# Six slot plans of a fused RWKV-6 and GELU-MLP kernel, each put in a new order

## The chip, the cores and the metric

The kernel runs on one core of a Trainium2 chip. Its time is the device time of one execution in microseconds (us), and the figure for a kernel is the median of several runs. A profile is a separate execution, recorded by the hardware. The engines are PE (TensorE, the matrix engine; PEld is its weight load), DVE (VectorE), ACT (ScalarE), POOL (GpSimd) and SP (SyncE, which here issues nearly all DMAs). Every engine works through its own queue of instructions in the order in which the program recorded them, and waits at an instruction until what it needs is there.

## The reference

First comes a linear-attention recurrence over 768 time steps for 4 batches and 8 heads of 48 channels, in float32:

```python
for t in range(S):
    cur = einsum('bhd,bhe->bhde', u * k[t], v[t])
    y[t] = einsum('bhd,bhde->bhe', r[t], state + cur)
    state = w[t][..., None] * state + einsum('bhd,bhe->bhde', k[t], v[t])
```

The heads are then laid side by side to a matrix `x` of 3072 rows and 384 columns, and an MLP follows with the exact GELU: `gelu(x @ w_in) @ w_out`, 384 to 2048 to 384.

## The kernel before, in words

The 3072 rows are cut into eight blocks of 384 (T), two for each batch; block `x` is half `x % 2` of its batch. Attention of a block works on chunks of 64 steps (C). Its output `xT` is the input of the MLP of the same block. The two are pipelined: in stage `x` (L1390 to L1416) the MLP of block `x - 1` is recorded together with the attention of block `x`, and the last MLP stands alone behind the stages.

**Slots and plans.** `attention(x, unit)` (L366 ff) and `mlp(x)` (L982 ff) are Python generators. Each `yield` ends a slot, which is a handful of instructions. `PLAN[x]` is a string that stands in the source; each letter takes the next slot from one stream and so records its instructions next on their engines:

```python
streams = {".": mlp(x - 1), "s": slots, "f": following, "l": load(x + 1, nc.sync), ...}
for c in PLAN[x]:
    next(streams[c], None)
for c in ".slxw" if x == 0 else ".slxwc":
    while next(streams[c], streams) is not streams:
        pass
slots = following
```

`.` is the MLP, `s` the rest of this block's attention, `f` the start of the next block's attention, `l` the loads of the next block, `x` five or ten sums of `xT` that the next MLP needs, `w` sums of weights (stages 2 and 7 only). A letter whose stream is at its end does nothing. Slots of one stream keep their order, so a plan only decides how the streams are interleaved, and with that the order in every engine's queue. "Stage 2" to "stage 7" below go by the key of the plan; they are the third to eighth stage.

**The attention slots of blocks 2 to 7**, with the names used in this document:

| name | work | lines |
|---|---|---|
| A0 | four products r*u*k on DVE; needs the loads of r and k | L404 |
| A1 to A11 | products and sums on DVE over r, k and the decays w | L391, L398, L424, L432 |
| Q0 | ACT copies r (plain), DVE scales it into `kx` (lay out) | L573, L578, L579 |
| Q1, Q2, Q4 | three bursts of 64x64 matmuls into pairs of PSUM banks (`d`); Q4 also has small ones | L604, L595 |
| Q3, Q9, Q10 | DVE copies the three bursts under masks into `a_sb` | L637 |
| Q5, Q6, Q7 | DVE updates r and k; Q6 has the ACT copies for Q8 | L658, L665, L669, L573 |
| Q8 | lay out again, for the second round | L578, L579 |
| Q11, Q12 | two masked DVE copies of the small matmuls | L687 |
| R1, R2, R4 | the bursts of the second round; in even blocks R1 holds all three | L604 |
| R3, R10, R11 | ACT copies their rows, six or twelve copies each | L620 |
| R5 to R7 | DVE updates r and k | L658, L665, L669 |
| R8, R9 | four DVE transposes of k and then twelve small DMAs, the moves, on SP (eight and four) | L552, L547 |
| K1 | four ACT copies of k's diagonal blocks | L733 |
| KV | 64x64 matmuls of k and v, into both pairs of banks | L749 |
| S1 to S3 | 20 DVE steps that chain the states out of these banks | L764 |
| I | matmuls into `y_ps` (both pairs again), and a fence: a tiny DVE copy | L790, L802 |
| Y | more matmuls into `y_ps`, held behind the fence; six ACT copies and six DMAs to `xT` | L832, L855, L862 |

There are two pairs of banks, used in turn. So a burst waits until the copies of the burst before the last are done, I waits for the end of S3, and R4 waits for R3.

**The MLP slots.** `h_halves` (L1011 to L1083) computes the hidden layer with seven products for each of four groups of blocks; its slots are called first, third, seventh, second, fifth, sixth and fourth, and run for q = 0 to 3. Each has four or eight 192-column matmul records, an ACT copy or GELU, and in third and seventh a DVE addition (L1065, L1083). Then come the output products (L1237), two slots of eight records each, in this order: 00, 11, 01, s2, s1, s3, s2w. After them an odd block has five more products (E11, Es2, Es1, Es3, Es2w; L1342 to L1360) and an even one two (al0, al1; L1331, L1334). `of_g` (L1003 to L1007) makes sums of GELUs on DVE. The hidden slots and the products share two PSUM banks, so the first slots of a stage wait until the last products of the stage before have been added or copied (L1360, L1334).

Q0 to Q12 of a stage are among its `s`; A0 to A9 may come as `f` of the stage before. Loads have ten slots: three for r, three for w, three for k and one for v, 256 KB each but the last.

Of the kernel before, what the change touches and what calls it, by code (L numbers as in the profile page):

```python
# [41 lines left out]
        ".cswc.ccc.cccss.lc.ccscs..cc.cs.cclwcsc.ccssc.c.cccsccc..ssccc.c.lcls.cc.ccsc.w.clwscclccc"  # L42
        ".c.swcw.ss.ccs.lcsc..cwcccslccslff..w..fw.wfs..f..flffffffww"
    ),
    2: "...l...s..ws.swssswssss.sslsw...ssss.sssws.ll..ws.w..lw.sw.wl.sls.sls..lf.s....sf..f.f.xx.fxl.x.x",
    3: "l..sss..s.s..s.s....s...s.ssllss.sss.s.s.ss.l..lsss..sssss.sls.s..s......s..ls.llssf.sf.sflf.f.x.x..xxfffxf",
    4: "...s...lsl......s.s....sss..ssss..s..ss..s..s...llssslss....s.slss...s...sll.sl.s.sfs..fsf.ff..xl.x.xfffxffx",
    5: ".l..........ls.ss...s.sslls.ssss..ss.sls...sss..sssssl.ss.s..s.......s.lssll.sfsf.f.s.ff.x..x.xxxl",
    6: "sss.sls.....s......ls.s....s.sssssss..s.....s.ss....s.s.ssss.s.l.ss.l.ls.l...s.l.lslssf..s.ffs..lff.xx..xffxffx",
    7: "......s.s....s.s...s.ssssss...sss.ss...sss..ssss.s...ss.ww.ww.wwsw.ww.ww.ws.s.ss.s.ww.swww.swwwwwwww.wwww.www.xxxx.xxxxxx",  # L50
}


# [1423 lines left out]
```

## Time and profile before

| what | us |
|---|---|
| median of 3 runs (588.08 to 589.55) | 589.5 |
| the profiled execution | 592.28 |
| its span, first to last instruction | 590.5 |
| PE busy | 571.7 (97%) |
| DVE busy | 462.9 (78%) |
| ACT busy | 275.9 (47%) |
| mean granted TensorE clock | 1.000 |

The span is the time from the first to the last instruction on the core; the execution takes 1.8 us more. A matmul in float32 is recorded as two matmuls, and their recorded ends overlap, so the distance from one start to the next says more than the duration: 192 columns follow each other every 0.163 us. Some records are missing.

### The profile page before, as it was taken

How to read it: one execution, taken by the hardware profiler on the slowest of the kernel's cores; microseconds unless marked ns; L12 is line 12 of the kernel's file. 1: busy time of each engine (PE TensorE's matmuls, PEld its weight loads, DVE VectorE, ACT ScalarE, POOL GpSimd, SP SyncE). 2: the span in 40 equal slices, each digit the busy share in tenths (PEclk: the TensorE clock that was granted, in tenths of full speed). 3: DMA queues.
4: the chain of work that ended last, by engine and by line, in shares of the span. 5: the costliest groups of instructions: out<-in, count | busy, mean ns of one | idle time of the engine just before them, and what ended most of it. 6: DMA issues, size and time to landing. Idle time of an engine off the chain costs nothing. (4 is left out here: it accounts for less than half of the span.)

```text
span 590.5 us, 17425 instructions
## 1 busy us (share of the span) xinstructions
PE 571.7 (97%) x7505; PEld 508.1 (86%) x7517; DVE 462.9 (78%) x907; ACT 275.9 (47%) x640; POOL 8.0 (1%) x21
## 2 busy tenths in 40 slices
PE   7769999999999999999999999999999999999998
PEld 3566666766799999999999999999998999999997
DVE  7879767988968986787859987688758998975532
ACT  2458889323612558046461468145560465523400
POOL 3100000000000000000000000000000000000000
PEclk9999999999999999999999999999999999999999
DMA  7649661120142301341023311330015200210000
GB/s 245 206 138 354 211 232 56 34 88 2 29 139 78 109 3 31 98 125 38 1 42 104 122 38 21 93 115 7 3 31 163 73 2 2 41 39 8 1 14 33
DMA packets 51004, 46.80 MB, mean 79 GB/s; under 512 B 31728, under 2 KB 36080, under 8 KB 50928
## 3 DMA queue, kind: packets, MB, share of 16 engines
q1 hardware_dynamic: 50832, 45.62, 25.4%
q8 instruction: 59, 0.97, 0.7%
q14 instruction: 17, 0.14, 0.1%
q10 hardware_dynamic: 96, 0.07, 0.1%
HBM read 36.24 MB, written 4.72 MB: 69 GB/s over the span
## 5 line engine op out<-in xcount | busy, mean ns | idle before, releaser
L1011 PE MATMUL h_ps<-xT,w_in_sb 128*128 128x192 f32 x408 | 81.2, 330 | 0.7 <-DVE o_sb L1360 0.6
L1011 PEld LDWEIGHTS h_ps<-xT,w_in_sb 128*128 128x128 f32 x408 | 67.8, 190 | 3.7 <-ACT g L1043 1.2
L1223 PE MATMUL h_ps<-xT,w_in_sb 128*128 128x384 f32 x192 | 64.1, 490 | 0.1
L1223 PEld LDWEIGHTS h_ps<-xT,w_in_sb 128*128 128x128 f32 x192 | 35.9, 190 | 23.9
L1237 PE MATMUL o_ps<-w_out_sb,g 128*128 128x192 f32 x224 | 39.5, 326 | 0.0
L1237 PEld LDWEIGHTS o_ps<-w_out_sb,g 128*128 128x128 f32 x224 | 36.9, 190 | 0.3
L620 ACT COPY a_sb<-d 32x256 f32<-32x256 f32 (+8 forms) x90 | 32.6, 362 | 4.6 <-PE d L604 3.1
L1237 PE MATMUL o_ps<-w_out_sb,f 128*128 128x192 f32 x176 | 31.7, 330 | 0.0
L1237 PE MATMUL o_ps<-t,g 128*128 128x192 f32 x176 | 31.4, 329 | 0.0
L1237 PE MATMUL o_ps<-w_out_sb,e 128*128 128x192 f32 x176 | 31.3, 328 | 0.0
L1237 PE MATMUL o_ps<-t,s 128*128 128x192 f32 x176 | 30.9, 327 | 0.0
L1237 PE MATMUL o_ps<-t,e 128*128 128x192 f32 x176 | 30.9, 327 | 0.0
L637 DVE COPY_PREDICATED a_sb<-quarter,d 128x480 f32<-128x480 uint8 (+5 forms) x54 | 23.1, 437 | 8.6 <-PE d L604 7.3
L465 PEld LDWEIGHTS d<-rkw 64*64 64x64 f32 x1152 | 19.1, 134 | 12.2 <-issue 8.5
L764 DVE SCALAR_TENSOR_TENSOR st<-st,tot_sb,kv_ps 128x48 f32<-128x48 f32 x160 | 28.9, 257 | 0.9 <-PE kv_ps L749 0.8
L1011 PE MATMUL u_ps<-s,w_in_sb 128*128 128x192 f32 x160 | 29.5, 327 | 0.0
L1237 PEld LDWEIGHTS o_ps<-t,g 128*128 128x128 f32 x176 | 28.7, 190 | 0.4
L1237 PEld LDWEIGHTS o_ps<-w_out_sb,e 128*128 128x128 f32 x176 | 28.8, 190 | 0.3
L1237 PEld LDWEIGHTS o_ps<-w_out_sb,f 128*128 128x128 f32 x176 | 28.7, 190 | 0.4
L1237 PEld LDWEIGHTS o_ps<-t,s 128*128 128x128 f32 x176 | 28.8, 190 | 0.1
L1237 PEld LDWEIGHTS o_ps<-t,e 128*128 128x128 f32 x176 | 28.8, 190 | 0.1
L604 PE MATMUL d<-kx,rkw 64*64 64x96 f32 x1056 | 28.2, 248 | 0.0
(236 smaller groups left out, 1163.6 us busy)
## 6 DMA issues: line engine op xcount, KB each, us to landing
rkw<-in_rkw_dram SPq DMA_DIRECT2D x54, 256.0 KB, 4.0
raw<-in_w_out_dram SPq DMA_DIRECT2D x8, 768.0 KB, 5.2
v_in<-in_v_dram SPq DMA_DIRECT2D x8, 584.0 KB, 4.1
raw<-in_w_in_dram SPq DMA_DIRECT2D x5, 768.0 KB, 8.8
out_dram<-o_sb SPq DMA_DIRECT2D x20, 192.0 KB, 2.2
rkw<-kx SPq DMA_DIRECT2D x72, 48.0 KB, 2.0
rkw<-in_rkw_dram SPq DMA_DIRECT2D x6, 384.0 KB, 5.7
raw<-in_w_in_dram SPq DMA_DIRECT2D x9, 256.0 KB, 3.3
```

What stands on the lines that cost most here:

```text
L465: nc.tensor.matmul(d[half[p], g, n * width:(n + 1) * width], lhsT=kc[half[g], b, i, p], rhs=right(half[g], b, i, p), start=True, stop=True)
L604: nc.tensor.matmul(o[half[p], i * 3 * C // 2:(i + 1) * 3 * C // 2], lhsT=kc[half[g], n // NI, n % NI, p], rhs=rx[half[g], 2 * n + p], star ...
L620: nc.scalar.copy(out=at[z, g, first:behind, (a + 1) * h:], in_=d[z, :, :, to] if g == slice(None) else d[z, :, to])
L637: nc.vector.copy_predicated(out=an[:, :, :, :, (a + 1) * h:], mask=mask.to_broadcast(data.shape), data=data)
L764: nc.vector.scalar_tensor_tensor(out=stq[:, q, c], in0=stq[:, q, c - 1] if c else b4[:, q, NC - 1], scalar=totq[:, q, c:c + 1], in1=kvs[q ...
L1011: nc.tensor.matmul(o, lhsT=lhsT, rhs=rhs, start=start, stop=True, skip_group_check=True)
L1223: nc.tensor.matmul(h_ps, lhsT=w_in_sb[:, f // FI, j, f % FI * 128:(f % FI + 1) * 128], rhs=xT[:, j, :], start=(j == 0), stop=(j == NJ - 1))
L1237: nc.tensor.matmul(o, lhsT=lhs(j), rhs=rhs(j), start=start and j == 0, stop=(j == HF - 1), skip_group_check=True)
```

## The change

Six strings of `PLAN` are replaced. Every stream still gives the same slots in the same order, and the letters `f` are as many in each plan as before (5, 9, 10, 5 and 9 in stages 2 to 6), so no slot changes its stage. The new strings contain a few letters (`c`, and `w` in stages 3 to 6, and some behind the end of a stream) that find an empty stream and record nothing. Two slots that the old plan of stage 2 left to the loop behind it, and one of stage 7, are now named in the plan.

```diff
-    2: "...l...s..ws.swssswssss.sslsw...ssss.sssws.ll..ws.w..lw.sw.wl.sls.sls..lf.s....sf..f.f.xx.fxl.x.x",
-    3: "l..sss..s.s..s.s....s...s.ssllss.sss.s.s.ss.l..lsss..sssss.sls.s..s......s..ls.llssf.sf.sflf.f.x.x..xxfffxf",
-    4: "...s...lsl......s.s....sss..ssss..s..ss..s..s...llssslss....s.slss...s...sll.sl.s.sfs..fsf.ff..xl.x.xfffxffx",
-    5: ".l..........ls.ss...s.sslls.ssss..ss.sls...sss..sssssl.ss.s..s.......s.lssll.sfsf.f.s.ff.x..x.xxxl",
-    6: "sss.sls.....s......ls.s....s.sssssss..s.....s.ss....s.s.ssss.s.l.ss.l.ls.l...s.l.lslssf..s.ffs..lff.xx..xffxffx",
-    7: "......s.s....s.s...s.ssssss...sss.ss...sss..ssss.s...ss.ww.ww.wwsw.ww.ww.ws.s.ss.s.ww.swww.swwwwwwww.wwww.www.xxxx.xxxxxx",
+    2: ".....s.ww..w.sww.wslsssssslss.l...sssssswscss...s..s..w..wwsl.ll.s.lsswls..l...ss.sff...fxfx.fxll....xxx.",
+    3: (
+        "..ssssss.....l.....llss...s.sssssss..ss..ss.l...sss.sssslss....ss......lcsssslls..s.lf.s.f"
+        "f.ff..lxx..xxffw.ffxxsl"
+    ),
+    4: (
+        "l......c......s.s..s...s...s.sss..sssslw.ssss....s.s..sll..ssss.ss.l.....sslsls..l.lsfslf."
+        "ssf...ffx..xl.xfxxffxf.f"
+    ),
+    5: "......s.....cs.s...sss.sss..s.sss.ss....sss.slssssls.s.s.....s...sllwsssl..llllfsl..fs.f....fxxf.xxsxx.l",
+    6: (
+        ".s....ss.ss.ss......s....lss.ssssss.....sllsss.......ssssssl......sss....ll.ssss..llslf.s."
+        "ff.s..ff..xx.xwfscflxxlff.x"
+    ),
+    7: (
+        ".....s...ss....s...sss.ssss.ss.sss.....lsssw..wssssssw...s..w.s...wwwscwww.sss.ws.w.swwsww"
+        ".wws.w.x.xxxxxxxxx.wwwwwwxwww.w.wwwww."
+    ),
```

## The prediction, on record before the change was run

> **What bounds the kernel now.** I read the page first, then the busy times by stage (stages 2 to 7 one below the other), then the waits of PE in that stretch, then the timeline around each wait.
>
> ```profile
> span 590.5 us, 17425 instructions
> PE 571.7 (97%) x7505; PEld 508.1 (86%) x7517; DVE 462.9 (78%) x907; ACT 275.9 (47%) x640; POOL 8.0 (1%) x21
> ```
>
> ```profile
> 120.00:192.60 72.60, 72.56 (x784) 57.79 (x785) 63.44 (x121) 24.68 (x63) 0.00 (x0) 1.00 0.23 68
> 192.60:256.90 64.30, 64.30 (x835) 61.24 (x834) 51.87 (x95) 32.35 (x84) 0.00 (x0) 1.00 0.23 60
> 256.90:329.20 72.30, 71.79 (x869) 69.19 (x868) 59.39 (x113) 33.17 (x83) 0.00 (x0) 1.00 0.22 61
> 329.20:392.80 63.60, 63.27 (x830) 60.38 (x829) 51.45 (x95) 32.32 (x84) 0.00 (x0) 1.00 0.25 68
> 392.80:465.20 72.40, 70.96 (x866) 68.42 (x865) 57.99 (x110) 33.04 (x83) 0.00 (x0) 1.00 0.23 63
> 465.20:529.90 64.70, 64.14 (x835) 61.13 (x834) 58.15 (x119) 32.42 (x84) 0.00 (x0) 1.00 0.12 32
> ```
>
> ```profile
> PE y_ps L832 <- DVE fence L802: 1.3, 1, 1.3
> PE h_ps L1011 <- DVE o_sb L1360: 0.6, 1, 0.6
> PE kv_ps L749 <- DMA rkw<-kx: 0.5, 1, 0.5
> PE y_ps L790 <- DVE st L764: 0.3, 1, 0.3
> PE h_ps L1011 <- DVE o_sb L1334: 0.2, 1, 0.2
> ```
>
> ```profile
> 42.03 0.22 DVE L800 COPY fence<-y_ps 128x1 f32<-128x1 f32 x2
> 42.30 1.38 PE L832 MATMUL y_ps<-rkw,st 64*64 64x64 f32 x39 [0.49 <-DVE fence L800]
> ...
> 219.31 2.04 PE L604 MATMUL d<-kx,rkw 64*64 64x96 f32 x80
> 220.43 2.60 ACT L620 COPY a_sb<-d 32x320 f32<-32x320 f32 x6 [0.30 <-PE d L604]
> 223.43 0.56 PE L604 MATMUL d<-kx,rkw 64*64 64x96 f32 x16
> ...
> 297.34 1.96 DVE L552 STREAM_TRANSPOSE kx<-rkw 128x384 f32<-128x384 f32 x4
> 310.52 1.74 PE L749 MATMUL kv_ps<-v_in,rkw 64*64 64x48 f32 x92 [0.51 <-DMA rkw<-kx]
> ...
> 380.30 1.63 PE L790 MATMUL y_ps<-a_sb,v_in 64*64 64x64 f32 x96 [0.33 <-DVE st L764]
> 453.93 3.01 DVE L404 SCALAR_TENSOR_TENSOR kx<-rkw,u_sb 128x384 f32<-128x384 f32 x4 [1.73 <-DMA out_dram<-o_sb]
> ```
>
> The first column pair of the stage rows is length and PE busy: over 410 us, PE is idle for 2.9 us. So the old plans already keep PE fed, and a new order can only win back the few waits listed, while each link that it tightens becomes a wait of PE. From start to start I find some 6 us in stages 2 to 7 that are not matmul pitch: Y of stage 6 1.3, KV of stage 4 0.95 and of stage 3 0.3, the starts of stages 7, 6, 4 and 3 together 1.8, I of stage 5 0.4, R2 in each odd stage 0.16, Q4 in each odd stage 0.2.
>
> **The change part by part.** Nothing is added, so only waits and mode changes count. I compared, link by link, what PE has to do between two slots with what DVE, ACT and SP need between them.
>
> *Mode changes.* Y follows I without other matmuls in stages 2 and 7; all other mergers cancel (39 runs of 64x64 matmuls become 37). Eight 192-column records between I and Y take 1.50 us instead of 1.30, and the first 64x64 load has 0.16 to 0.23 in front, so a pair costs 0.2 to 0.36: together -0.4 to -0.7, I take -0.6. [...]
>
> *I directly before Y.* The matmuls between them covered the fence. Without cover the only row is stage 0: 0.49 us of PE idle. Bounds 0.3 (the fence's 0.2 and a hand-over) and 0.7 (start to start in that row); two times 0.5, +1.0.
>
> *R4 in stages 3, 5 and 7.* R4 needs the bank of R1, which the six copies of R3 free. They start 1.12 us after R1 and last 2.60, so 3.7 us after R1. PE's cover was R1 and R2 1.8, sixth 0.65, fourth 1.3, mode change 0.2: 3.95. In stages 3 and 5 sixth now stands before R1: 3.3, late by 0.4. In stage 7 the cover stays, but Q11 and Q12 (1.92) now stand before third's addition on DVE, a GELU in second3 waits for it, and R3 behind it on ACT starts 0.9 later: late by 0.5. Bounds 0 (ACT finds slack) and 0.6; +1.3 for three. In return R2 no longer meets Q12: three times 0.16, -0.5.
>
> *I behind S.* I needs both pairs back from S3, 3.2 us after KV's end with 20 steps (stage 5: 377.10 to 380.30), 4.8 in stage 6 (447.45, S to 452.2). Stage 3 drops from 5.4 to 2.8 us of cover, +0.4. Stage 6 drops from 5.4 to 4.1, +0.7. Bounds 0 and 1.2. Stage 5 stays at its 0.4.
>
> *Stage 4.* Q1 and Q4 come 4 us later among the matmuls, R1 1.3 earlier. Q0's second half waits for ACT copies behind fourth1: Q1 late by 0.35. From Q4's end DVE then does Q6 to Q12 in 8.9 (Q8 waiting for copies behind sixth3), two additions 1.0, six sums 4.0, R5 1.35, R6 and R7 2.0, R8 1.95: 19.2. The moves take 9.3 more (twelve at 0.66, the last landing 2.0 after its issue), 28.5. PE's work from Q4 to KV is 27.2. KV so waits 1.3 in place of 0.95, and Y 0.2 behind its fence: +0.85 in all. Bounds -0.9 (DVE has slack) and +2.
>
> *Stage 5.* Between KV and A0 DVE gets L1291 (1.28). A0 ends 7.5 after KV's end, the fence at 7.7, Y is due at 7.55: +0.2. All ten loads but two now stand behind the moves on SP, so four of w and r go out just ahead of k's three. In stage 6 of before just this had k land 6.0 us after issue, against 3.3 in stage 5. I take +0.2 for it, between 0 and 1.5.
>
> *Stage 6.* R9's four moves stand behind one load only, and two loads instead of four go out before k's: A0 no longer waits 1.73, so Y's 1.3 goes. DVE is done earlier, so L1360 no longer holds stage 7: -0.7. Sum -2.0, bounds -2.1 and 0.
>
> *The rest.* KV of stage 3 lost 0.3 to moves that landed late; now K1's copies end with the last matmul before it, there and in stage 7: -0.3 and +0.1. Later loads, weight sums and A-slots I cost at nothing: the five or more matmul slots beside them cover each; without that cover a DVE slot is 0.5 to 2.4.
>
> *Sum.* -0.6 +1.0 +1.3 -0.5 +1.1 +0.85 +0.4 -2.0 -0.2 = +1.35. Two of the gains are waits after DMAs that landed 1.8 us late; such landings (306.52 to 310.38, 2.0 being usual) come in four of six stages and hit a wait twice, and can hit others: +0.65. Total +2.0. On the profiled execution (590.5 span, 592.28 in all) that is 594.3; it is 2.8 above the median, so against 589.5 I say 591.5.
>
> **The rivals.**
>
> *The ends of the stages decide: faster.* Y stands 1.3 us earlier before the stage's end in stages 3, 4 and 5, and 3.9 in stage 7, so `xT` lands and the last banks are free in time. For it: L1360 and L1334 and the late `xT` (sx0 waits 1.40 in stage 5) are what holds the starts of stages. Then all 1.8 of the starts and Y's 1.3 go, with -0.6, -0.5 and -0.95 for KV in stage 4 (-5.15), and +3.4 of R4, I and fence stays if ACT and DVE are as late as the rows say (-1.75); with two of the three R4 waits hidden +2.5 stays: -2.6, 586.9. From that point it decides. Against it: stage 5 gets A4 (2.2) between sx1 and L1334, which gives the start of stage 6 its 0.5 back.
>
> *Waits only change places: the same.* For it: every plan has the same DVE sum per stage and PE is at 99% here. Between -1.7 and +1.7; 590.
>
> *k's loads and the moves land late.* In stages 4 and 5 KV and A0 have nothing left. One late landing in each and one in stage 7 adds 1.8 each to the +1.35: 596. Against it: only two of four hit a wait before. [...]
>
> A plan that does nothing is excluded: the order of PE's and DVE's queues differs in every stage.
>
> **How the numbers follow.** My forecast, small losses between +1.8 and +4.5, has 0.40; the late landings 0.12; the same 0.28; faster 0.20. What a measurement can tell from no change is 0.3%, 1.8 us. That makes slower 0.52, same 0.28, faster 0.20. The range runs from 587.6, which cuts off about half of the faster case, to 595.0, short of the late one, and leaves out about 0.2. The slower case alone is 591.3 to 594.0.
>
> **What would show it.** R4 idle 0.3 to 0.6 before L604 in three stages; L832 idle 0.5 behind L802 in stages 2 and 7; L790 behind L764 in stages 3 and 6; KV of stage 4 behind the moves; Y of stage 6 and the start of stage 7 without a wait; PE busy time as before. It is wrong if those idle times are missing, or if a stage's start waits where I see none.

## The result and the profile after

The new order is slower. Four runs of each gave 594.39 us (592.82 to 595.21) against 589.01 (588.08 to 589.55), a ratio of 1.009 with the interval 1.0062 to 1.0118. A longer comparison, eleven runs against 34, gave 592.65 against 589.43, a ratio of 1.0052 (1.0035 to 1.0069), which is +3.1 us (2.1 to 4.1). The mean clock granted in a run does not make this difference: among its runs with 1.000 the medians are 591.89 (five) and 588.46 (eleven), among those with 0.997 they are 593.59 (six) and 589.74 (fifteen), 3.4 and 3.8 apart. The forecast was 591.5, slower by 2.0. The profiled execution of the new kernel took 593.81 us, 1.5 more than that of before.

The page's first lines, and the busy times from stage start to stage start (stages 2 to 7; a stage starts here with the first 128x192 matmul of its MLP, stage 2 with the one 128x512 matmul just before its MLP), for the new kernel; columns as in the prediction:

```profile
span 592.0 us, 17424 instructions
PE 570.4 (96%) x7505; PEld 507.5 (86%) x7517; DVE 462.6 (78%) x907; ACT 275.9 (47%) x640; POOL 8.0 (1%) x21
...
119.53:192.80 73.27, 73.05 (x787) 58.22 (x786) 62.77 (x117) 24.67 (x63) 0.00 (x0) 1.00 0.24 67
192.80:257.65 64.85, 64.06 (x834) 60.99 (x833) 52.45 (x98) 32.38 (x84) 0.00 (x0) 1.00 0.24 64
257.65:330.17 72.52, 71.34 (x867) 68.73 (x866) 58.75 (x111) 32.95 (x83) 0.00 (x0) 1.00 0.23 65
330.17:394.81 64.64, 63.77 (x833) 60.86 (x833) 51.73 (x97) 32.37 (x84) 0.00 (x0) 1.00 0.25 70
394.81:466.10 71.29, 70.92 (x866) 68.41 (x865) 58.97 (x111) 33.10 (x83) 0.00 (x0) 1.00 0.20 52
466.10:531.25 65.15, 63.83 (x834) 61.03 (x833) 57.75 (x114) 32.30 (x84) 0.00 (x0) 1.00 0.13 33
```

The busy times of all engines are those of before within 1.5 us, as they must be with the same slots; PE's idle time in the six stages went from 2.9 to 4.8 us. The waits of PE in that stretch (what waited, for whom, us in total, times, longest), and where they stand in the timeline:

```profile
PE d L616 <- ACT a_sb L632: 1.3, 3, 0.5
PE y_ps L802 <- DVE st L776: 1.0, 3, 0.4
PE y_ps L844 <- DVE fence L814: 0.9, 3, 0.6
PE kv_ps L761 <- DMA rkw<-kx: 0.6, 2, 0.4
PE y_ps L844 <- issue: 0.5, 1, 0.5
```

```profile
311.64 0.34 PE L761 MATMUL kv_ps<-v_in,rkw 64*64 64x48 f32 x9 [0.38 <-DMA rkw<-kx]
320.92 0.31 PE L844 MATMUL y_ps<-rkw,st 64*64 64x64 f32 x4 [0.56 <-DVE fence L814]
...
361.17 0.56 PE L616 MATMUL d<-kx,rkw 64*64 64x96 f32 x16 [0.39 <-ACT a_sb L632]
453.82 0.59 PE L802 MATMUL y_ps<-a_sb,v_in 64*64 64x64 f32 x25 [0.37 <-DVE st L776]
...
517.91 1.63 PE L802 MATMUL y_ps<-a_sb,v_in 64*64 64x64 f32 x96
519.72 1.02 PE L844 MATMUL y_ps<-rkw,st 64*64 64x64 f32 x48 [0.18 <-DVE fence L814]
521.19 0.93 PE L844 MATMUL y_ps<-rkw,st 64*64 64x64 f32 x48 [0.46 <-issue]
```

R4 (L616) waits for ACT's copies in stages 3, 5 and 7, I (L802) for the states (L776) in 3, 5 and 6, KV and Y in stage 4, and in stage 7 Y stops half way, 48 matmuls in, for nothing that the profile names. A line with a bracket gives idle time of PE; counted from one matmul's start to the next, less its usual pitch, the same waits are 0.1 to 0.2 longer.

### The profile page after: what moved, and what is told of

The parts are those of the page before. It is cut to its first block, busy times and chain, and to the rows that moved or that the text cites. A ratio compares the mean times of both kernels' runs of the same rounds, so it can differ in the third digit from the quotient of the medians.

```text
span 592.0 us, 17424 instructions
## 1 busy us (share of the span) xinstructions
PE 570.4 (96%) x7505; PEld 507.5 (86%) x7517; DVE 462.6 (78%) x907; ACT 275.9 (47%) x640; POOL 8.0 (1%) x21
## 4 chain that ended last, share of the span: by engine, by line
PE 58%; DVE 6%; ACT 1%; DMA 1%; issue 0%; SPq 0%; DVEq 0%
PE o_ps L1249 24%; PE h_ps L1023 15%; PE u_ps L1023 11%; PE d L616 3%; DVE st L776 2%; PE c_ps L1023 2%; PE y_ps L844 1%; ACT a_sb L632 1%; PE kv_ps L761 1%; PE y_ps L802 1%; DMA rkw<-in_rkw_dram 1%; DVE a_sb L649 1%; DVE kx L416 1%; PE d L607 0%; DMA rkw<-kx 0%
## 5 line engine op out<-in xcount | busy, mean ns | idle before, releaser
L776 DVE SCALAR_TENSOR_TENSOR st<-st,tot_sb,kv_ps 128x48 f32<-128x48 f32 x160 | 29.1, 256 | 2.3 <-PE kv_ps L761 2.2
L1238 ACT ACTIVATE g<-h_ps 128x256 f32<-128x256 f32 (+1 forms) x32 | 13.9, 433 | 31.6 <-PE h_ps L1235 31.2
L616 PE MATMUL d<-kx,rkw 64*64 64x96 f32 x1056 | 27.3, 247 | 1.3 <-ACT a_sb L632 1.3
```

The costliest lines, as they stand in the source:

```text
L616: nc.tensor.matmul(o[half[p], i * 3 * C // 2:(i + 1) * 3 * C // 2], lhsT=kc[half[g], n // NI, n % NI, p], rhs=rx[half[g], 2 * n + p], star ...
L776: nc.vector.scalar_tensor_tensor(out=stq[:, q, c], in0=stq[:, q, c - 1] if c else b4[:, q, NC - 1], scalar=totq[:, q, c:c + 1], in1=kvs[q ...
L1238: nc.scalar.activation(out=gs[group][:, f % FG, 0:t], in_=h_ps[:, 0:t], func=AF.Gelu)
```

## The experiments

**Each order once more.** The profiled execution of before was 2.8 us above its median; which of its waits does a usual execution hold? Both kernels ran again, and so did two mixtures:

```diff
-    2: ".....s.ww..w.sww.wslsssssslss.l...sssssswscss...s..s..w..wwsl.ll.s.lsswls..l...ss.sff...fxfx.fxll....xxx.",
+    2: "...l...s..ws.swssswssss.sslsw...ssss.sssws.ll..ws.w..lw.sw.wl.sls.sls..lf.s....sf..f.f.xx.fxl.x.x",
...
```

That is new357 in its first line, the new plans with 2, 4 and 6 from before; new246 has 3, 5 and 7 from before and 2, 4 and 6 new.

> The old plans unchanged, a second execution. Theory (waits of the old order come and go): the profiled execution of 592.28 held waits after late DMA landings that most executions do not hold, so this one has Y of stage 6 under 0.3 idle instead of 1.34 and the start of stage 7 under 0.4 instead of 0.72; span 586.5 to 588.5, ratio 1.000. Rival (granted clock): the waits are all there again, some 6 us in stages 2 to 7, the span is 590 to 591, and what separates the times of the two kernels is the clock granted in the timed runs (1.000 here against 0.994 for the new order).

> The new plans unchanged, a second execution. Theory: R4 waits 0.46, 0.46 and 0.62 in stages 3, 5 and 7, Y 0.5 to 0.6 behind the fence in stages 2, 5 and 7, I 0.4 behind S3 in stages 3, 5 and 6, as in the first execution, within 0.1 each, since they come from engines' fixed durations; only the two waits of KV behind the moves vary; time 594, ratio 1.009. Rival (granted clock): the same waits, but the ratio falls to about 1.003, the 1.5 us of the two first profiles, in runs where both kernels get the same clock.

> The new plans in stages 3, 5 and 7, the old ones in 2, 4 and 6. Theory: R4 waits (1.5), I behind S3 in stage 3 (0.4) and the fences of stages 5 and 7 (1.1), less R2 and the two mode changes (0.8): +2.5 over before, with those waits as long as in the new order, and stages 2, 4 and 6 as long as in the old. Rival (the stage's start decides): a stage's loss is taken over by the stage behind it, and 4 or 6 get longer by over 0.5 at their starts.

> The new plans in stages 2, 4 and 6, the old ones in 3, 5 and 7. Theory: fence of stage 2 (0.5) less two mode changes (0.3), the starts and Q1 of stage 4 (0.8), I behind S3 in stage 6 (0.4): +1.0 to +2.0 over before's typical execution, no R4 wait, R2 waits 0.16 in stages 3, 5, 7 as before. Rival (stage 6 was the loss of the old order in every execution): its 1.3 of Y and 0.7 of the start of stage 7 go, and the time is 0.5 to 1 below before.

Measured (medians; ratios to runs of before in the same comparison, with the 95% interval): before again 588.98 us (ratio 0.9984, 0.9967 to 1.0001), the new order 592.65 (1.0052, 1.0035 to 1.0069), new357 592.66 (1.0043, 1.0024 to 1.0062), new246 591.6 (1.0029, 1.0007 to 1.0050). Length of each stage in the traces, in us:

| stage | 2 | 3 | 4 | 5 | 6 | 7 | sum |
|---|---|---|---|---|---|---|---|
| before, first | 73.12 | 64.14 | 71.70 | 64.24 | 72.42 | 64.51 | 410.13 |
| before, again | 73.12 | 64.14 | 71.20 | 64.34 | 70.99 | 64.50 | 408.29 |
| new, first | 73.27 | 64.85 | 72.52 | 64.64 | 71.29 | 65.15 | 411.72 |
| new, again | 73.27 | 64.61 | 72.52 | 64.64 | 71.70 | 65.54 | 412.28 |
| new357 | 73.13 | 64.60 | 71.14 | 64.66 | 71.25 | 65.50 | 410.28 |
| new246 | 73.27 | 64.00 | 73.00 | 64.25 | 71.19 | 63.86 | 409.57 |

The second execution of before has these waits of PE in stages 2 to 7:

```profile
PE y_ps L790 <- DVE st L764: 0.6, 2, 0.3
PE h_ps L1011 <- DVE o_sb L1360: 0.6, 1, 0.6
PE y_ps L832 <- DVE fence L802: 0.2, 1, 0.2
```

and the second of the new order these:

```profile
PE d L616 <- ACT a_sb L632: 1.4, 3, 0.6
PE y_ps L844 <- issue: 1.2, 2, 0.7
PE y_ps L802 <- DVE st L776: 1.0, 3, 0.4
PE h_ps L1023 <- DVE o_sb L1346: 0.4, 1, 0.4
PE kv_ps L761 <- DMA rkw<-kx: 0.4, 1, 0.4
PE y_ps L844 <- DVE fence L814: 0.4, 2, 0.2
```

Y of stage 6, which waited 1.34 in the first execution of before, waits 0.18 in the second, and KV of stage 4, which lost 0.95, loses 0.06; the start of stage 7, expected below 0.4, waits 0.7 in both. The second has waits of its own: 0.23 for Y of stage 3 and 0.38 for I of stage 4. So two of the waits that the sum started from are not in every execution. R4's and I's waits are the same in both executions of the new order, within 0.02, as expected; the ratio came out between the 1.009 of the theory and the 1.003 of its rival. A stage keeps most of its length from mixture to mixture with its plan, but not all: the old stage 7 behind the new 6 is 0.64 shorter, the old 6 behind the new 5 is 0.26 longer than in the second execution of before. (In two expectations "stage 5" stands for Y's wait at 319 to 320 us, which is in stage 4.) Against the second execution of before, the two mixtures add 2.0 and 1.3 us in the sum, 3.3 together, where the whole new order adds 3.4 and 4.0. The rival of the clock falls: the second trace of before has the clock 0.997, as has that of the new order, with 408.3 against 412.3, and the times differ by 3.4 and 3.8 among runs of the same clock.

**R4's cover given back.** Sixth3 goes behind R3 in stages 3 and 5, Q11 and Q12 behind third2 in stage 7:

```diff
-    3: "..ssssss.....l.....llss...s.sssssss..ss..ss.l...sss.sssslss....ss......lcsssslls..s.lf.s.ff.ff..lxx..xxffw.ffxxsl",
+    3: "..ssssss.....l.....llss...s.sssssss..ss..ss.l..sss..sssslss....ss......lcsssslls..s.lf.s.ff.ff..lxx..xxffw.ffxxsl",
-    5: "......s.....cs.s...sss.sss..s.sss.ss....sss.slssssls.s.s.....s...sllwsssl..llllfsl..fs.f....fxxf.xxsxx.l",
+    5: "......s.....cs.s...sss.sss..s.sss.ss...sss..slssssls.s.s.....s...sllwsssl..llllfsl..fs.f....fxxf.xxsxx.l",
-    7: ".....s...ss....s...sss.ssss.ss.sss.....lsssw..wssssssw...s..w.s...wwwscwww.sss.ws.w.swwsww.wws.w.x.xxxxxxxxx.wwwwwwxwww.w.wwwww.",
+    7: ".....s...ss....s...sss.ssss.ss.s..ss...lsssw..wssssssw...s..w.s...wwwscwww.sss.ws.w.swwsww.wws.w.x.xxxxxxxxx.wwwwwwxwww.w.wwwww.",
```

> The new plans, but sixth3 stands behind R3 again in stages 3 and 5, and Q11 and Q12 behind third2 again in stage 7. Theory (R4 waits for the six copies of R3, and its cover was cut): the idle time before R4 (0.46, 0.46, 0.62) falls below 0.15 in all three stages, R2 meets Q12 again in stages 3 and 5 (0.17 each); stages 3, 5 and 7 shorter by 0.3, 0.3 and 0.6: 1.2 less in all. Rival (the copies are late for another reason, so the order of the slots is not it): R4 still waits over 0.3 in at least two stages.

Measured: 592.26 us (1.0057, 1.0031 to 1.0082). R4 no longer stands among the waits of PE, of which these are the largest:

```profile
PE y_ps L802 <- DVE st L776: 1.0, 3, 0.4
PE y_ps L844 <- DVE fence L814: 1.0, 3, 0.6
PE y_ps L844 <- issue: 0.7, 1, 0.7
...
```

Stages 3, 5 and 7 take 64.29, 64.41 and 64.98: 0.32, 0.23 and 0.56 less than in the second execution of the new order, 1.1 in all, and R2 meets Q12 again, with 0.16 in each of the three. That is the step as predicted, the detour in stage 7 over third's addition, the GELU and R3's copies among it. The time cannot tell 1.1 us; the traces can.

**The wait inside Y.** Two kernels: a product slot between I and Y, and 128 instructions more at the start of PE's stream.

First the slot (apart), then the instructions (shift):

```diff
-    2: ".....s.ww..w.sww.wslsssssslss.l...sssssswscss...s..s..w..wwsl.ll.s.lsswls..l...ss.sff...fxfx.fxll....xxx.",
+    2: ".....s.ww..w.sww.wslsssssslss.l...sssssswscss...s..s..w..wwsl.ll.s.lsswls..l...s.ssff...fxfx.fxll....xxx.",
-    7: ".....s...ss....s...sss.ssss.ss.sss.....lsssw..wssssssw...s..w.s...wwwscwww.sss.ws.w.swwsww.wws.w.x.xxxxxxxxx.wwwwwwxwww.w.wwwww.",
+    7: ".....s...ss....s...sss.ssss.ss.sss.....lsssw..wssssssw...s..w.s...wwwscwww.sss.ws.w.sww.swwwws.w.x.xxxxxxxxx.wwwwwwxwww.w.wwwww.",
```

```diff
-    def keep_warm(n, elsewhere=False):
+    def keep_warm(n, elsewhere=False, few=0):
...
+        for _ in range(few):
+            nc.tensor.matmul(t[:, 0:16], lhsT=zeros[:, 0:128], rhs=zeros[:, 0:16], start=True, stop=True)
...
-    keep_warm(16)
+    keep_warm(16, few=64)
```

> The new plans, but one product slot (8 matmuls, 1.3 us) stands between I and Y in stages 2 and 7. Three theories for the wait in the middle of Y of stage 7 (0.67 and 0.89 in two executions, put down to issue; Y's first half waits 0.2 to 0.4). Fence alone: both fences are done before Y's first matmul, so nothing changes in the middle; only the start of Y moves up, by 0.2 to 0.4 in each stage. Instruction fetch (I and Y are 384 instructions of PE in 3.2 us, and PE goes on 1.3 to 1.5 us after the end of a 16 KB instruction packet): the wait in the middle falls below 0.2 and stage 7 (65.2 to 65.5) is shorter by 0.5 to 1.0. Late data of the second half (S3 or r): the wait keeps its end, and Y ends at the same distance from S3 as before. Stage 2 keeps its 73.2 within 0.2: the fence's 0.39 goes, a mode change of 0.2 to 0.36 comes.

> The new plans, and 64 matmuls of 16 columns more at the very start, where PE waits for the first loads: 128 instructions more in PE's stream, which move every boundary of a 256-instruction block by half a block against the work of stages 2 to 7. Instruction fetch: the wait 48 matmuls into Y of stage 7 (0.67 to 0.89) goes, or moves to another matmul, or changes by over 0.4, and so does the 0.70 in Y of stage 5; R4, I behind S3 and the fence of stage 2 keep their idle times within 0.1. Rival (a semaphore or late data): the waits stand before the same matmuls with the same length.

Measured: apart 593.34 us (1.0065, 1.0024 to 1.0105), shift 596.88 (1.0143, 1.0078 to 1.0208, two runs; its stage 2 starts 2.7 later than in the second execution of the new order, so the start with the 64 matmuls has a price of its own). I and Y of stage 7, first in the kernel apart, then in shift:

```profile
518.28 1.63 PE L802 MATMUL y_ps<-a_sb,v_in 64*64 64x64 f32 x96
519.84 1.57 PE L1249 MATMUL o_ps<-t,s 128*128 128x192 f32 x8
521.33 1.63 PE L844 MATMUL y_ps<-rkw,st 64*64 64x64 f32 x96
```

```profile
520.99 1.63 PE L804 MATMUL y_ps<-a_sb,v_in 64*64 64x64 f32 x96
522.80 1.72 PE L846 MATMUL y_ps<-rkw,st 64*64 64x64 f32 x96 [0.18 <-DVE fence L816]
```

Both take the stop in the middle away; stage 7 falls to 64.49 and 64.46, from 65.15 and 65.54. In shift I and Y still stand next to each other, with the same data and the same fences, so neither late data nor a semaphore is the cause; what the 128 instructions moved is the stream of PE's instructions. The profile lists DMA packets of 16 KB of the kind instruction on queue 8, 59 of them (0.97 MB) in the first execution of the new order and 60 in shift. That trace has 15,177 instructions of PE (15,022 matmuls and weight loads, and 155 of its sequencer), 257 for each of the 59; from this number, and from the 128 more instructions that went with one more packet, I take these packets for PE's instructions. In shift those nearest to this Y end at 518.24 and 523.89. The traces hold seven such stops inside a Y, one of them in stage 4, and each ends 1.3 to 1.5 us after the end of such a packet (in the first execution of the new order the packet stands from 518.93 to 519.87 and Y goes on at 521.19). In the second execution of the new order the packet of stage 7 is here, and no data moves beside it:

```profile
DMA packets 1, 0.02 MB, mean 14 GB/s; under 512 B 0, under 2 KB 0, under 8 KB 0
...
q8 instruction: 1, 0.02, 5.6%
```

This is the window from 518.2 to 519.4; the last matmul before the stop starts at 519.98, the next at 520.87. I and Y are 384 instructions of PE in 3.2 us, one and a half times the 257 of a packet; over the 592 us of the first execution PE has 26 in a microsecond, here 120. The stops are 0.5 to 0.9 us long from start to start. That PE waits there for its next instructions is my reading of the packets and of shift: the trace itself names nothing that PE waits for.

Apart lost in stage 2 what it won in stage 7: 74.36 instead of 73.27. There Y, and xT with it, came a slot later, while the slots that read xT stayed where they were: DVE stood 1.55 us before the transfer with a product's operation queued behind, and PE 0.61 for that:

```profile
187.64 0.36 DVE L946 TENSOR_TENSOR s<-xT 128x192 f32<-128x192 f32 x1 [1.55 <-DMA xT<-ysb]
...
190.03 2.19 PE L1249 MATMUL o_ps<-w_out_sb,e 128*128 128x192 f32 x12 [0.61 <-DVE e L1362]
```

Shift did not come out shorter in the sum (412.27): stage 5 went from 64.64 to 66.02, with KV 1.4 longer behind late moves. Two of these, issued at 373.68 and 374.31, landed 4.28 and 3.84 us later, and the shift had put an instruction packet beside them, from 374.31 to 376.07. This led to the next test.

**Stage 4, and the moves that land late.**

Stage 4 gets its old first half, up to fourth2 (q4_early); the same and the 64 small matmuls at the start are q4_early_shift:

```diff
-    4: "l......c......s.s..s...s...s.sss..sssslw.ssss....s.s..sll..ssss.ss.l.....sslsls..l.lsfslf.ssf...ffx..xl.xfxxffxf.f",
+    4: "...s...lsl......s.s....sss..ssss..s..ss..ss....s.s..sll..ssss.ss.l.....sslsls..l.lsfslf.ssf...ffx..xl.xfxxffxf.f",
```

> The new plans, but stage 4 has the old order up to fourth2 (Q1 to Q10 some 4 us earlier among the matmuls, A9 to A11 and two loads as before), and the new one behind it. Theory (from Q4 on DVE and SP's twelve moves are the chain that KV of stage 4 waits for): KV's waits of 0.73 to 1.06 fall below 0.2; stage 4 goes from 72.5 to 71.5 to 71.8. Rival (the moves land late whatever DVE does): KV still waits 0.5 or more, and the last move's landing stands over 2.5 behind its issue.

> The old first half of stage 4 and the 64 small matmuls at the start, together. Theory: in the run with the old first half KV of stage 4 waited 0.90 only because one move of 12, issued 0.97 before a 16 KB instruction packet of 1.47 us, landed 3.62 after its issue instead of 2.0; without that it would have landed 0.7 before KV. With the stream shifted by half a block (in the run with the shift alone the packets of stage 4 stood at 297.29 and 315.67, none beside the last moves) KV waits below 0.2, stage 4 takes 71.6 to 72.2, and every move that overlaps no instruction packet lands within 2.9. Rival (the new second half of stage 4 makes the moves late, or late landings come by chance): KV waits 0.5 or more again, and late landings stand where no instruction packet is.

Measured: q4_early 592.13 us (1.0063, 1.0042 to 1.0084), and against the expectation KV of stage 4 still waits, 0.90 in one piece, and stage 4 takes 73.14. But not because of the chain: the last move is issued at 304.80, 2.8 before KV, and lands only at 308.42. In the window from its predecessor's issue (304.7 to 307.4) the DMA view of this kernel shows an instruction packet beside the last two moves; in the window before it (301.9 to 304.9) there is none. The last column is the median from issue to landing:

```profile
q8 instruction: 1, 0.02, 3.4%
...
rkw<-kx SPq DMA_DIRECT2D x2, 48.0 KB, 2.8
```

```profile
q1 hardware_dynamic: 1751, 0.22, 42.0%
issues: line engine op xcount, KB each, median us to landing
rkw<-kx SPq DMA_DIRECT2D x6, 48.0 KB, 2.0
```

With the stream shifted (q4_early_shift, 595.44 us, 1.0119, 1.0079 to 1.0158, two runs, again with the price of the small matmuls) KV of stage 4 runs through, and stage 4 takes 72.02, with 0.44 before I and 0.86 before Y:

```profile
312.17 1.61 PE L763 MATMUL kv_ps<-v_in,rkw 64*64 64x48 f32 x96
```

So with the stream shifted the old first half takes KV's wait away, as the step had it. Y's wait of stage 4 stays: with the one slot that the new plan leaves between I and Y instead of two, the fence behind A0 keeps PE idle for 0.6 to 1.4 in seven of the eight executions with this second half, and in each A0 (L404 of before) has stood 0.4 to 1.7 for k's loads.

**A better mixture.** Each stage has its own best plan, and I can be moved a slot away from S3:

Mix, against before (in stage 6 the new plan with I one slot later):

```diff
-    4: "...s...lsl......s.s....sss..ssss..s..ss..s..s...llssslss....s.slss...s...sll.sl.s.sfs..fsf.ff..xl.x.xfffxffx",
+    4: "...s...lsl......s.s....sss..ssss..s..ss..s..s...llssslss....s.slss...s...sll.sl.s.sf.s.fsf.ff..xl.x.xfffxffx",
-    5: ".l..........ls.ss...s.sslls.ssss..ss.sls...sss..sssssl.ss.s..s.......s.lssll.sfsf.f.s.ff.x..x.xxxl",
+    5: ".l..........ls.ss...s.sslls.ssss..ss.sls...sss..sssssl.ss.s..s.......s.lssll.sff.sf.s.ff.x..x.xxxl",
-    6: "sss.sls.....s......ls.s....s.sssssss..s.....s.ss....s.s.ssss.s.l.ss.l.ls.l...s.l.lslssf..s.ffs..lff.xx..xffxffx",
+    6: ".s....ss.ss.ss......s....lss.ssssss.....sllsss.......ssssssl......sss....ll.ssss..llslf..sff.s..ff..xx.xwfscflxxlff.x",
```

Mix_r2, against mix (sixth3 before R1 and seventh3 before R4, in 5 and 7 as shown for 3):

```diff
-    3: "l..sss..s.s..s.s....s...s.ssllss.sss.s.s.ss.l..lsss..sssss.sls.s..s......s..ls.llssf.sf.sflf.f.x.x..xxfffxf",
+    3: "l..sss..s.s..s.s....s...s.ssllss.sss.s.s.ss.l..l.sss..ssssssls.s..s......s..ls.llssf.sf.sflf.f.x.x..xxfffxf",
...
```

Mix2, against mix (A1 behind I):

```diff
-    5: ".l..........ls.ss...s.sslls.ssss..ss.sls...sss..sssssl.ss.s..s.......s.lssll.sff.sf.s.ff.x..x.xxxl",
+    5: ".l..........ls.ss...s.sslls.ssss..ss.sls...sss..sssssl.ss.s..s.......s.lssll.sf.sff.s.ff.x..x.xxxl",
```

> The old plans in stages 2, 3 and 7, the old plans of 4 and 5 with I one product slot later, and the new plan of stage 6 with I one slot later. Theory (each stage's waits are its own plan's): I no longer waits behind S3 (0.38 to 0.40 in stages 4 and 5, 0.44 in the new 6), the start of stage 7 (0.71) goes; stage lengths 73.1, 64.1, 70.9 to 71.3, 63.9, 70.8, 63.9, sum 406.7 to 407.3 against 408.3 and 410.1 of before's two executions: 1.0 to 1.6 less than before, ratio 0.9975. Rival (waits change places): the fence of Y, with one slot of cover less, takes back what I gains; sum 408 or more, ratio 1.000.

> The mixed plans, and in stages 3, 5 and 7 sixth3 ahead of R1 (as in the new order) and seventh3 ahead of R4. Theory: R2 no longer meets Q12 (0.17 in each), and R4 keeps its cover of 3.9 (R1 and R2 1.8, fourth2 1.3, seventh3 0.65, mode change 0.2), so it does not wait: 0.5 less than the mixed plans, ratio 0.9965. Rival: R5 to R8 come 0.65 later on DVE and SP, and KV of stages 3, 5 or 7 or R4 itself waits over 0.3, which takes the 0.5 back.

> The mixed plans again, but in stage 5 A1 (the 1.78 us sum) comes after I, so that the fence of Y no longer stands behind it on DVE. Theory: A0 ends 3.1 us after S3, the fence with it, 0.8 before Y is due, so Y's 2.14 and the slow products behind it (stage 5 took 68.2) go: stage 5 takes 63.9, the sum of stages 2 to 7 is 407.0 to 407.8 against 408.3 and 410.1 of before's two executions; ratio 0.998, between 0.996 and 1.000. Rival (the old plans have no waits left that a move of I can win): the sum is 408.3 or more, ratio 1.000 or above.

Measured: mix 590.77 us (1.0037, 1.0014 to 1.0060), mix_r2 598.55 (1.0174, 1.0140 to 1.0208), mix2 587.24 (0.9967, 0.9953 to 0.9982). In mix, I waits behind S3 in no stage any more, as the theory had it, but stage 5 lost 3.9 us (68.24): with I moved behind A1, its fence stands behind A1's sum on DVE, and Y with it. DVE and PE there, and then the busy times of a window behind that wait:

```profile
379.00 3.06 DVE L416 SCALAR_TENSOR_TENSOR kx<-rkw,u_sb,rkw 128x384 f32<-128x384 f32 x4
382.09 1.78 DVE L403 TRANSPOSE_TENSOR_REDUCE rkw<-kx 128x48 f32<-128x1536 f32 x1
...
384.76 0.22 DVE L814 COPY fence<-y_ps 128x2 f32<-128x2 f32 x2
...
384.97 2.76 PE L844 MATMUL y_ps<-rkw,st 64*64 64x64 f32 x96 [2.07 <-DVE fence L814]
...
385.30:388.60 3.30, 3.30 (x95) 3.18 (x86) 1.11 (x2) 0.83 (x2) 0.00 (x0) 0.50 0.18 65
```

The wait is only 2.1 us of the loss. Right behind it the granted clock, third from the end in the last line, is 0.50 for 3.4 us (385.23 to 388.64); Y takes 2.76 instead of 1.63, and half of 3.4 us, some 1.7 by this estimate, is lost there. 1.7 of 590 us is 0.3%, so by the same estimate a mean clock of 0.997 is one such stretch, and 0.994, which this execution had, is two. One follows Y's wait of 2.02 in stage 5 of mix_r2, but nothing of the kind follows KV's wait of 2.22 in its stage 3, so whether a wait brings it about is not shown.

Mix_r2 lost 5.3 more (stages 2 to 7 417.19 against 411.90). Seventh3's addition (L1095) waits for an ACT copy that stands behind R3's six, and R5 (L670) now stands behind the addition on DVE, so R5 starts at 224.42 instead of 218.72 and the first move at 229.77 instead of 227.03 (the stage itself begins 0.6 later), KV of stage 3 waits 2.9, and stages 5 and 7 are 0.7 and 2.3 longer too. In these lines of mix_r2 the first is an earlier one of these additions, and R5 starts right behind the second:

```profile
218.88 0.55 DVE L1095 TENSOR_TENSOR g<-g,o_sb 128x384 f32<-128x384 f32 x1
223.95 0.56 DVE L1095 TENSOR_TENSOR g<-g,o_sb 128x384 f32<-128x384 f32 x1 [4.52 <-ACT o_sb L1059]
224.42 1.35 DVE L670 TENSOR_TENSOR rkw<-kx,tot_sb 128x1152 f32<-128x1152 f32 x1
```

Mix2 differs from mix in one pair of letters. Its stages take 73.11, 63.88, 70.75, 64.47, 70.75 and 64.16, 407.12 in all, 1.2 less than the second execution of before and 3.0 less than the first; the theory's range was met, though stage 5 missed its 63.9. PE has these waits left:

```profile
PE h_ps L1023 <- DVE o_sb L1372: 0.4, 2, 0.2
PE y_ps L844 <- DVE fence L814: 0.2, 1, 0.2
```

In the times it beats the new order, but whether it beats before is open. All nine runs of mix2 had the clock 1.000, and of the fourteen of before beside them only five; among runs of that clock it is 587.24 against 587.87, a difference that the spread of the runs (586.16 to 588.58, and 587.07 to 589.07) does not carry.

## Why the prediction was right, and where it was off

*The direction and most of its causes were right*: nothing but waits changed, and most stand where the steps put them. R4: 1.3 predicted, 1.5 from start to start in both executions (1.3 and 1.4 idle), 1.1 net when undone (R2's three times 0.16, the predicted gain, come back with it). I behind S: 0.4 in stage 3 as predicted, 0.44 in stage 6 instead of 0.7, 0.4 unchanged in stage 5. Stage 2: +0.2 predicted from the fence and the mode changes, +0.15 measured. The start of stage 7: its 0.7 went (0.05 and 0.2 left).

*The size was low, and the step that failed is stage 6 with the last line of the sum.* I let waits of the one profiled execution go as gains of the change, above all Y's 1.3 of stage 6, and then subtracted the 2.8 by which that execution stood above the median. The second execution of before takes 1.8 less in stages 2 to 7 (408.29 against 410.13), with 0.18 for Y of stage 6 and no KV wait in stage 4: these waits are among the 2.8. What was taken off with the execution could not be won by the change as well. With the 1.8 put back the same sum gives +3.8, against +3.1 (2.1 to 4.1) in the longer comparison, and +3.4 and +4.0 for the new traces against the second of before. That this comes so near is in part luck, since the terms below are off both ways.

*Sizes off within that.* Stage 7's I and Y side by side: the fence costs 0.36 from start to start (0.2 idle), there and in stage 2, near its lower bound of 0.3 and not the 0.5 taken, but Y's stop half way, 0.64 and 0.86 in the two executions, was in no row of before. Stage 4: 72.52 against 72.55 predicted (71.70 and 0.85; the three parts add up to 0.9), but the match is luck, for the parts are others: KV 1.2 and 0.85 (counted as the 0.95 of before) instead of 1.3, Y 0.6 and 0.8 instead of 0.2, Q1 nothing instead of 0.35. Y's 0.6 is the fence behind k's loads, for which A0 stands 0.80; most of the 0.8 is one of the seven stops inside a Y. Stage 5: Y and k's loads, +0.4, did not come (0.08 and 0.07); what came in the second execution is 0.56 at the start of stage 6, behind L1334 of before (L1346), where the prediction had expected the start's wait to come back.

*The rivals.* That the ends of the stages decide fell: the start of stage 7 went, but R4, I and the fences all stayed, and stage 6 got a start of its own to wait for. That waits only change places fell in the longer comparison, whose interval begins at 1.0035. Late landings were taken as chance, 0.65; those of the moves stand beside instruction packets, below, and cost KV 0.95 and 1.4 in two experiments, but nothing in the new order's own two executions, where KV of stage 4 resumes 0.13 behind a move that took its usual 2.0.

## What to carry to other kernels

A wait in one profiled execution is not yet a wait of the kernel: profile the old kernel twice before a change is credited with removing one, and never subtract an execution's excess from a sum that already spends it. In an order of slots the cover of a link is counted in PE time between its two ends, but a slot that moves takes its operations on every in-order queue along: the two longest waits here (2.1 us in stage 5 of mix, 2.9 in stage 3 of mix_r2) came from one DVE operation that got in front of another, not from a cover that was too thin. With PE at 99%, a moved letter won 0.2 to 0.6 us in a stage here and could lose 3. Stages can be put together from different plans, with an eye on the start of the next. And before two times are compared at this level, compare runs of the same granted clock (the medians of before at 1.000 and at 0.997 are 1.3 us apart).

## What the runs showed of the hardware that I had not expected

*Moves beside a packet of instructions landed later.* Over the 14 profiled executions the traces record the landing of 969 moves of 48 KB (L547, L559 and L561). Of these, 871 had no 16 KB instruction packet under way between 0.3 and 2.0 us after their issue: their median is 2.02 us, and none took more than 2.91. With such a packet (98 moves) the median is 2.96, the longest 4.28, and all 46 moves that took over 3 us are among them; these landed 1.0 to 2.1 us after the packet's end. The first executions of before and of the new order alone have 144 moves: 127 without a packet, median 2.02 and none over 2.87, and 17 with one, median 2.78 and up to 3.86, with all seven that took over 3 us among them. Loads beside them are not the reason: 87 of the 98 had no load and no output DMA in flight in that time, and their median is 2.96 as well; some 270 of the 871 had one, with a median of 2.02. For the 24 KB DMAs into xT in stages 2 to 7 it is the same: 377 without a packet, none over 1.93; 115 with one, median 2.48, up to 3.86 (in the same two executions 56, none over 1.92, and 16, median 2.37, up to 3.57). What I had called late landings by chance is of this kind: the move from 306.52 to 310.38 in the first trace of before stands beside a packet from 307.79 to 309.30. Why a move beside a packet lands late is not shown: no trace here shows the DMA engines one by one.

*PE stopped inside bursts of small matmuls.* The 96 matmuls of 64x64 in a Y that runs through, with their weight loads, take 1.56 us up to the next product (384.65 to 386.21 in stage 5 of before), two instructions in 16 ns; at that rate the 257 of a packet would last 2.1 us, an estimate. Two such bursts with one product slot between them or none stopped PE for 0.5 to 0.9 in five of the kernels, and with the 128 instructions more at the program's start no Y stopped so. So an edit at the start of a program changed waits 370 and 500 us later, one by +1.4 us and one by -0.9: by these two, a part of what separates two kernels at this level is where their packets of instructions fall.
